# Output product of a pair of tiles with seven half-size products, and one pool of 2 KB tiles

## The chip, the cores and the metric

The kernel runs on one core of one Trainium2 chip. The metric is the time of one execution on the device in microseconds (us), measured over repeated runs. An execution taken by the hardware profiler is looked at beside it; it has a time of its own.

## What is computed

A chunked attention is followed by a gated feed-forward layer with a norm in front. All arrays are float32; the feed-forward weights arrive as raw 64-bit words and are converted on the chip.

```python
# q, k, v: 8 batches x 8 heads x 576 tokens x 64; chunks of 64 tokens
scores = scale * np.matmul(q_c, k_c.transpose(0, 1, 2, 4, 3))
attn = softmax(scores)                    # row by row
x = (attn @ v_c) laid out as 4608 tokens x 512
rms = np.sqrt(np.mean(x * x, axis=-1, keepdims=True) + 1e-06)
xn = x / rms * rms_g
g = xn @ w_gate                           # 512 -> 1536
silu = g * (1.0 / (1.0 + np.exp(-g)))
val = xn @ w_val                          # 512 -> 1536
return (silu * val @ w_out)               # 1536 -> 512
```

## The kernel before

**Precision.** A float32 operand is split into a rounded part (hi, float32r) and the rest (lo), and each product is made of three matmuls: hi x hi, hi x lo, lo x hi. A split takes a cast on ScalarE (for instance L739, `gh`) and a subtraction on VectorE (L740, `gl`).

**Tiles.** The 4608 tokens make nine tiles of 512. The first three are worked off plainly, one after the other (the loop over PLAIN). Tile 0 also converts the weights. Tile 1 also prepares seven combinations of each block of the up weights (`sides`: sums on GpSimd at L544, casts on ScalarE at L572, subtractions on VectorE at L574) and stores them in memory outside the core. In these tiles each of twelve feature blocks goes through `gated` (two up products of 12 matmuls, silu, multiplication, split at L494 and L498) and then `down` (L506). The six remaining tiles make three pairs (the loop over b at L909).

**A pair, up.** `up_pair` works off six blocks of features. For each it makes seven products (P1, P5, P6, P2, P3, P7, P4) of half-size operands that stand in for the eight of a 2 x 2 block product, at 12 matmuls each (L637), with weights from the sides and x operands `xp` of which `x_side` made the hi and lo parts (L585, L586). Behind each product, `after` combines: VectorE reads one operand from PSUM (L700, L707, L713, and others), ScalarE copies and applies silu (L679), and GpSimd adds and multiplies operands in SBUF (L701, L705, L711, L717). The result `g` of a block is 128 features x (2 x 2) x 512 tokens in SBUF.

**A pair, output.** For each of the two tiles, 12 feature blocks go through `split_g` and `down`: 12 matmuls with a piece of g stationary (128x128) and the output weights moving (512 columns). That is 24 steps, 288 matmuls and 24 splits in a pair. The four sums in PSUM of each tile are copied by `evacuate` (L730 on ScalarE, L732 on VectorE) and stored as 256 KB pieces. Splits go through two tiles of the pool `gp`; other 2 KB pieces go through a pool `tmp` of four.

**Beside it.** While a pair is worked on, the attention of the next pair's tokens runs in small steps between products: a `Steps` object calls each from a table by step number (`PAIR_STEPS`). Its stages are: loads, scores and softmax, values (L356, on PE), normalization (L370, L423, L378) and a transposition (L384). In the second half of the output the next pair's x operands are scaled (L600), subtracted from each other (`less`, L603) and split (`x_side`).

**What sets the order.** TensorE's order is written out by hand (the program order inside `manual_schedule`). The other engines' orders come from a scheduler, in which `urgent()` raises splits and combinations. Every engine works off its queue strictly in order. All transfers are issued by one queue (SP), in order. Weights come in pieces of 1 MB, asked for three ahead (AHEAD_R for the up products' `wr`, AHEAD_O for the output's `wo`); the output weights are loaded twice per pair, 12 x 1 MB.

Of the kernel before, what the change touches and what calls it, by code (L numbers as in the profile page):

```python
# [17 lines left out]
P = 128  # L18
# [45 lines left out]
def tile_chunk_attn_swiglu(  # L64
# [68 lines left out]

    def tmp_tile(name):
        return tmp.tile([P, 512], F32, tag="tmp", name=name)

# [18 lines left out]
    def conv_join(n):  # L155
        if n < len(pairs):


            low, high, w = conv[n]
            wi = w.bitcast(I32)  # L160
            nc.vector.tensor_scalar(w, w, HIGH_LEAST, HIGH_MOST, op0=ALU.max, op1=ALU.min)
            nc.vector.tensor_single_scalar(wi, wi, 3, op=ALU.logical_shift_left)
            nc.vector.scalar_tensor_tensor(
                wi, high, -(2**31), wi, op0=ALU.bitwise_and, op1=ALU.bitwise_or
            )
            nc.vector.tensor_tensor(wi, wi, low, op=ALU.add)
# [11 lines left out]
            if kind == "up":  # L178
                nc.sync.dma_start(wfd[f], w)

# [5 lines left out]

    wfd = [dram.tile([P, 2 * DM], F32, name=f"wfd{n}") for n in range(NF)]
    conv_at = [0]

# [290 lines left out]
    def gated(f, at, then):  # L480
# [35 lines left out]
    wsd = [dram.tile([P, 2, 2 * 2 * KH], F32, name=f"wsd{n}") for n in range((7 * NPR + 1) // 2)]  # L516
    wod = [dram.tile([P, 4 * DM], F32, name=f"wod{n}") for n in range(NPR)]

# [3 lines left out]
    def save_side(i, p, part):  # L522

        n = 7 * i + p
        dst = wsd[n // 2][:, n % 2].rearrange("p (a m c) -> p a m c", a=2, m=2)
        nc.sync.dma_start(dst, part.bitcast(F32))

# [3 lines left out]
    def save_plain(i):  # L531

        one, two = parts_of(2 * i), parts_of(2 * i + 1)
        save_side(i, P1, one[:, :, :, :KH])
        save_side(i, P2, one[:, :, :, KH:])
        save_side(i, P4, two[:, :, :, KH:])
        nc.sync.dma_start(wod[i], flat(out_parts[i]).bitcast(F32))

    def sides(i, st):

        at = {}

        def total(out, one, two, op):
            nc.gpsimd.tensor_tensor(out, one, two, op=op)  # L544

        def load():
            for f in range(2):
                w = st.tile([P, 2, DM], F32, tag="ab", bufs=3, name="w")
                nc.sync.dma_start(w.rearrange("p m c -> p (m c)"), wfd[2 * i + f])
                for half in range(2):  # L550
                    at[f + 1, half + 1] = w[:, :, half * KH : (half + 1) * KH]

        def sums():
            total(at[2, 2], at[2, 1], at[2, 2], ALU.add)
            total(at[2, 1], at[1, 1], at[2, 1], ALU.subtract)
            total(at[1, 1], at[2, 2], at[1, 1], ALU.subtract)
            total(at[1, 2], at[1, 2], at[1, 1], ALU.subtract)

        def split():
            save_split(i, P7, at[2, 1])  # L560
            save_split(i, P5, at[2, 2])
            save_split(i, P6, at[1, 1])
            save_split(i, P3, at[1, 2])

        return [load, sums, split]

    def save_split(i, p, w):

        n = 7 * i + p
        dst = wsd[n // 2][:, n % 2].rearrange("p (a m c) -> p a m c", a=2, m=2)  # L570
        part = tmp.tile([P, 2, KH], F32R, tag="tmp", name="side")
        nc.scalar.copy(part, w)  # L572
        nc.sync.dma_start(dst[:, 0], part.bitcast(F32))
        nc.vector.tensor_tensor(w.bitcast(F32R), w, part.bitcast(F32), op=ALU.subtract)  # L574
        nc.sync.dma_start(dst[:, 1], w)

# [13 lines left out]
    def x_sides(x1, x2, st):  # L590
# [10 lines left out]

        def less(out, one, two):
            nc.vector.tensor_tensor(out, one, two, op=sub)  # L603

# [44 lines left out]
    def up_pair(i, step, wos):  # L649
# [8 lines left out]
        for k, p in enumerate(ORD if i else FIRST):  # L658
# [4 lines left out]
            for m in range(2):  # L663
                if p == P1:
                    bank_of(m, "a", ps_h)
                elif p in (P6, P5, P4):
                    bank_of(m, {P6: "b", P5: "c", P4: "d"}[p], ps_acc)
                b = ps[m][{P1: "a", P2: "a", P6: "b", P7: "b", P5: "c", P3: "c", P4: "d"}[p]]
                product(n, m, p, b, p in (P1, P6, P5, P4), p in (P2, P7, P3, P4))
            with urgent():  # L670
# [64 lines left out]
    def split_g(src):  # L735
        gh = gp.tile([P, TT], F32R, name="gh")
        gl = gp.tile([P, TT], F32R, name="gl")
        with urgent():
            nc.scalar.copy(gh, src)  # L739
            nc.vector.tensor_tensor(gl, src, gh.bitcast(F32), op=ALU.subtract)  # L740
        return gh, gl

    def out_load(i):
        t = big([P, 2, 2, DM], F32R, "wo")
        nc.sync.dma_start(flat(t).bitcast(F32), wod[i])
        return t

    def unit_steps(u, x):
# [85 lines left out]
    for t in range(PLAIN):  # L834
        if t == 1:
# [9 lines left out]
            for i in range(NPR):  # L845
                steps = sides(i, st)
# [62 lines left out]
    for b in range(NB):  # L909
        t = PLAIN + 2 * b  # L910
        at = {}
        if b + 1 < NB:
            u = 2 * t + 4
            for n in range(4):
                for k, f in enumerate(unit_steps(u + n, (x, x2)[n // 2])):
                    at.setdefault(4 + 10 * n + PAIR_STEPS[k], []).append(f)
        step = Steps(at)
        gs = []
        wos = {}
        order = [(h, i) for h in range(2) for i in range(NPR)]  # L920
        for i in range(NPR):
            gs.append(up_pair(i, step, wos))
        loaded[0] = 0
        made = []
        if b + 1 < NB:
            made = sum(x_sides(x, x2, st), [])
        split = {}

        def split_next(n):
            if n < 2 * len(order):  # L930
                h, i = order[n // 2]
                split[n] = split_g(gs[i][:, n % 2, h])

        split_next(0)
        for n, (h, i) in enumerate(order):
            if i == 0:

                acc = [bank(ps_h if h and s < 2 else ps_acc, f"acc{s}") for s in range(NSUB)]
            for k in range(n, min(n + AHEAD_O, len(order))):
                if k not in wos:  # L940
                    wos[k] = out_load(order[k][1])
            if n == len(order) - AHEAD_R and b + 1 < NB:
                ring_load_ahead(0)
            for j in range(2):
                split_next(2 * n + j + 1)
                down(acc, 2 * i + j, *split.pop(2 * n + j), wos[n])
                step()
                if step.n > 46 and made:
                    made.pop(0)()
            if i == NPR - 1:  # L950
                for s in range(NSUB):
                    evacuate(acc, t + h, s)
        for f in made:
            f()
    ordered.__exit__(None, None, None)
# [50 lines left out]
```

## Time and profile before

| what | value |
| --- | --- |
| median of 3 runs | 935.18 us (933.87 to 935.7) |
| the profiled execution | 936.39 us |
| its span | 934.6 us |
| TensorE busy | 905.9 us, 97% of the span |
| VectorE, ScalarE, GpSimd busy | 516.2, 431.5, 172.7 us |
| granted TensorE clock | 1.000 |
| output stages of the three pairs | 62.96, 62.95 (less their first 12 matmuls) and 65.29 us |

The profiled execution lies 1.79 us above its own span, and 1.21 us above the median. In the profile an engine counts as busy while it computes. PE is TensorE's matmuls, PEld its weight loads, DVE is VectorE, ACT ScalarE, POOL GpSimd, SP the engine that issues the transfers. A row of a group reads: line, engine, operation, output<-inputs, shape, number of instructions | busy us, mean ns of one | idle us of the engine just before them and what ended it.

### The profile page before, as it was taken

The page shows a single profiled execution, that of the slowest core. Times are in us where ns is not written, and L with a number is a line of the kernel's source. Part 1 is how long each engine was busy: PE and PEld are TensorE (multiplying, and loading weights), DVE is VectorE, ACT ScalarE, POOL GpSimd, SP SyncE. Part 2 cuts the span into 40 slices and gives each one's busy share as a digit, 9 for nine tenths or more (in the row PEclk, how much of TensorE's full clock was granted, in tenths as well). Part 3 has the DMA queues.
Part 4 walks back from the last instruction along what each step waited for, and adds up shares of the span by engine and source line. Part 5 has one row for each costly group of instructions (what it writes and reads, how often), then busy time and mean ns, then how long its engine had stood idle before and what let it go on. Part 6 is the DMA issues. An engine that isn't in the chain of part 4 may idle for free.

```text
span 934.6 us, 17360 instructions
## 1 busy us (share of the span) xinstructions
PE 905.9 (97%) x6936; PEld 742.2 (79%) x6936; DVE 516.2 (55%) x889; ACT 431.5 (46%) x697; POOL 172.7 (18%) x157
## 2 busy tenths in 40 slices
PE   4599999999999999999999999999999999999998
PEld 3478788888888788888888888888888888888886
DVE  5899983554546555754664735546656332333232
ACT  4999963453446543553444425445444223222222
POOL 0100012224200000233332002322330023224100
PEclk9999999999999999999999999999999999999999
DMA  8688998868975644767789666586987585337511
GB/s 338 248 310 309 329 367 318 264 236 250 308 275 150 187 148 154 270 218 280 253 288 348 269 269 256 213 289 188 335 311 265 239 329 211 135 135 296 243 46 46
DMA packets 78737, 231.84 MB, mean 248 GB/s; under 512 B 8384, under 2 KB 40128, under 8 KB 62912
## 3 DMA queue, kind: packets, MB, share of 16 engines
q1 hardware_dynamic: 78656, 230.72, 69.0%
q8 instruction: 55, 0.90, 0.4%
q14 instruction: 26, 0.21, 0.1%
HBM read 171.97 MB, written 58.72 MB: 247 GB/s over the span
## 4 chain that ended last, share of the span: by engine, by line
PE 85%; ACT 7%; DVE 4%; DMA 2%; issue 1%; SPq 1%; POOL 0%; ACTq 0%; DVEq 0%; POOLq 0%
PE acc L506 29%; PE ps_b L637 11%; PE ps_c L637 11%; PE ps_a L637 11%; PE ps_g L471 7%; PE ps_v L471 7%; PE ps_d L637 5%; PE ps_o L356 2%; PE ps_s L239 2%; ACT w L152 1%; ACT e L275 1%; ACT raw L153 1%; ACT parts L177 1%; DVE parts L185 1%; DMA x<-kT_dram 1%
## 5 line engine op out<-in xcount | busy, mean ns | idle before, releaser
L506 PE MATMUL acc<-wo,gh 128*128 128x512 f32 x576 | 177.6, 390 | 0.0
L506 PEld LDWEIGHTS acc<-wo,gh 128*128 128x128 f32 x576 | 108.0, 188 | 22.5
L506 PE MATMUL acc<-wo,gl 128*128 128x512 f32 x288 | 112.3, 390 | 0.0
L740 DVE TENSOR_TENSOR gl<-g,gh 128x512 fp32r<-128x512 f32 x72 | 49.7, 691 | 101.2 <-ACT gh L739 99.2
L637 PE MATMUL ps_b<-xp,wr 128*128 128x512 f32 x432 | 104.7, 391 | 0.0
L637 PE MATMUL ps_c<-xp,wr 128*128 128x512 f32 x432 | 104.3, 390 | 0.0
L637 PE MATMUL ps_a<-xp,wr 128*128 128x512 f32 x432 | 103.5, 390 | 0.0
L471 PE MATMUL ps_g<-xh,parts 128*128 128x512 f32 x288 | 97.1, 396 | 1.9 <-ACT sg L489 1.4
L739 ACT CAST gh<-g 128x512 fp32r<-128x512 f32 x72 | 44.8, 623 | 116.1 <-PE acc L506 110.9
L471 PE MATMUL ps_v<-xh,parts 128*128 128x512 f32 x288 | 95.7, 392 | 0.0
L637 PEld LDWEIGHTS ps_a<-xp,wr 128*128 128x128 f32 x432 | 80.9, 188 | 16.9
L637 PEld LDWEIGHTS ps_b<-xp,wr 128*128 128x128 f32 x432 | 80.6, 188 | 17.1
L637 PEld LDWEIGHTS ps_c<-xp,wr 128*128 128x128 f32 x432 | 80.8, 188 | 16.9
L506 PE MATMUL acc<-parts,gh 128*128 128x512 f32 x288 | 90.2, 394 | 0.0
L711 POOL TENSOR_TENSOR g<-u,u 128x512 f32<-128x512 f32 x18 | 23.2, 1289 | 342.1 <-DVE u L707 244.4
L423 POOL TENSOR_TENSOR ri<-ss,mhalf 128x1 f32<-128x1 f32 x36 | 23.7, 665 | 245.1 <-DVE ss L421 244.8
L471 PEld LDWEIGHTS ps_g<-xh,parts 128*128 128x128 f32 x288 | 54.3, 189 | 14.3 <-ACT sg L489 1.8
L471 PEld LDWEIGHTS ps_v<-xh,parts 128*128 128x128 f32 x288 | 54.5, 189 | 11.3
L506 PEld LDWEIGHTS acc<-wo,gl 128*128 128x128 f32 x288 | 54.1, 188 | 11.8 <-DVE gl L740 0.5
L506 PEld LDWEIGHTS acc<-parts,gh 128*128 128x128 f32 x288 | 53.3, 188 | 11.2
L506 PE MATMUL acc<-parts,gl 128*128 128x512 f32 x144 | 56.5, 392 | 0.0
L471 PE MATMUL ps_g<-xl,parts 128*128 128x512 f32 x144 | 56.4, 391 | 0.0
(105 smaller groups left out, 1393.2 us busy)
## 6 DMA issues: line engine op xcount, KB each, us to landing
wr<-wsd SPq DMA_DIRECT2D x63, 1024.0 KB, 7.8
wo<-wod SPq DMA_DIRECT2D x36, 1024.0 KB, 8.2
raw<-w_up_dram SPq DMA_DIRECT2D x12, 1024.0 KB, 9.4
vt<-v_dram SPq DMA_DIRECT2D x18, 512.0 KB, 6.7
wsd<-parts SPq DMA_DIRECT2D x18, 512.0 KB, 6.6
out_dram<-o SPq DMA_DIRECT2D x36, 256.0 KB, 2.2
qt<-qT_dram SPq DMA_DIRECT2D x17, 512.0 KB, 5.5
kt<-kT_dram SPq DMA_DIRECT2D x17, 512.0 KB, 5.9
```

Source lines behind the costliest of these rows:

```text
L152: nc.scalar.activation(w, high.bitcast(F32), AF.Abs, scale=2.0**16)
L153: nc.scalar.mul(low, low.bitcast(U32), 2.0**-29)
L177: nc.scalar.copy(parts[:, 0].rearrange("p i c -> p (i c)"), w)
L239: nc.tensor.matmul(st["s"][j][c * CH : (c + 1) * CH, pr], st["q"][rows, pr, tok : tok + CH], st["k"][rows, pr, tok : tok + CH], start=True ...
L356: nc.tensor.matmul(st["o"][(2 * c + t) * Q : (2 * c + t + 1) * Q, h * D : (h + 1) * D], eT[c][rows, t, h], vt[rows, c, h], start=True, sto ...
L423: nc.gpsimd.tensor_tensor(ri, ss, mhalf, op=ALU.pow)
L471: nc.tensor.matmul(ps, a[f][:, cols], b[dt], start=(dt == 0 and i == 0), stop=(dt == NDT - 1 and i == 2),)
L506: nc.tensor.matmul(acc[s], a[:, cols], b, start=(f == 0 and i == 0), stop=(f == NF - 1 and i == 2),)
L637: nc.tensor.matmul(ps, w[:, a, m, cols], xp[:, b, kt], start=start and kt == 0 and i == 0, stop=stop and kt == 1 and i == 2, skip_group_ch ...
L711: nc.gpsimd.tensor_tensor(g[:, 0, 1], kp["u2"], kept[0]["u2"], op=mult)
L739: nc.scalar.copy(gh, src)
L740: nc.vector.tensor_tensor(gl, src, gh.bitcast(F32), op=ALU.subtract)
```

## The change

**Output of a pair.** `down_pair` takes the place of `down` for the pairs. It makes the output product with seven half-size products too: 7 products x 6 blocks are 42 steps (n = 6p + i for product p and block i), each with two halves m and 3 matmuls, 252 matmuls in a pair. The output weights are now stationary (128x128, features of the output on partitions) and the split g moves (512 tokens). `down_after` combines the products: copies on ScalarE, four kinds of sums on VectorE from PSUM, one on GpSimd. The output is stored transposed in 8 pieces of 256 KB, and the host turns it back.

**Operands.** Each step splits one operand (cast L779, subtraction L780), two steps ahead (AHEAD_G). Behind the splits of P1, P5, P6 and P2, GpSimd writes the next operand over g in place (L809): 24 subtractions of 128x512 per pair.

**Pool.** One pool `tmp` of eight 2 KB tiles serves sg, gh, gl, o, side and the second half's u2 and p5, where there were two pools of (2 x 2) and 4.

**Output weights.** Tile 0 also stores the converted output weights (`wfo`), tile 2 makes their sides (`out_sides`: 4 sums of 128x256 on GpSimd, 4 casts, 4 subtractions and 8 stores for each of 6 blocks), and a pair loads them as 11 pieces of up to 1 MB.

**Beside it.** The units' steps come two steps earlier (2 + 10n for 4 + 10n), the x operands' at steps 44, 46, ..., and two of their subtractions of 128x1024 go from VectorE to GpSimd.

```diff
-    gp = ctx.enter_context(tc.tile_pool(name="gp", bufs=2))
-    tmp = ctx.enter_context(tc.tile_pool(name="tmp", bufs=4))
+    tmp = ctx.enter_context(tc.tile_pool(name="tmp", bufs=8))
...
     def split_g(src):
-        gh = gp.tile([P, TT], F32R, name="gh")
-        gl = gp.tile([P, TT], F32R, name="gl")
+        gh = tmp_tile("gh", F32R)
+        gl = tmp_tile("gl", F32R)
...
+    def down_pair(b, gs, wos, step):
...
+        sums = {P1: ((0, 0), (0, 1)), P5: ((0, 0), (1, 1)), P6: ((0, 1), (1, 1)), P2: ((1, 0), (0, 0))}
+        homes = {P1: (0, 0), P5: (0, 0), P6: (0, 0), P2: (1, 0), P3: (1, 1), P7: (0, 1), P4: (1, 0)}
...
+        def split_next(n):
+            if n >= 7 * NPR:
+                return
+            p, i = divmod(n, NPR)
+            g = gs[i]
+            split[n] = split_g(g[:, homes[p][0], homes[p][1]])
+            if p in sums:
+                (j, h), (j1, h1) = sums[p]
+                nc.gpsimd.tensor_tensor(g[:, j, h], g[:, j1, h1], g[:, j, h], op=ALU.subtract)
...
+        for n in range(AHEAD_G):
+            split_next(n)
+        for n in range(7 * NPR):
+            p, i = divmod(n, NPR)
+            for k in range(n // 4, min(n // 4 + AHEAD_O, NOS)):
+                if k not in wos:
+                    wos[k] = out_load(k)
...
+            for m in range(2):
...
+                for k, (a, c) in enumerate(((0, 0), (0, 1), (1, 0))):
+                    nc.tensor.matmul(
+                        ps[m][INTO[p]],
+                        w[:, a, m * P : (m + 1) * P],
+                        parts[c],
...
+            split_next(n + AHEAD_G)
+            if i == NPR - 1:
+                with urgent():
+                    for m in range(2):
+                        down_after(p, m, ps[m], kept[m], store)
+            step()
...
+            lambda: less(b12, b22, b12, nc.gpsimd),
             lambda: x_side(P6, t1),
+            lambda: less(b21, t1, b21, nc.gpsimd),
             lambda: x_side(P3, b22),
-            lambda: less(b12, b22, b12),
             lambda: x_side(P7, b12),
-            lambda: less(b21, t1, b21),
             lambda: x_side(P4, b21),
...
+            for i in range(NPR):
+                for k, f in zip((4, 6, 7), out_sides(i)):
+                    at.setdefault(3 * i + k, []).append(f)
```

**GpSimd's queue, end of the first pair's up products and start of its output.** The names are g (a block's result, six of them), u2, p5 and p1 (partial sums of the last block), ri (the norm of a unit). Before:

```order
L711 TENSOR_TENSOR g_5092<-u2_5150,u2_5148 128x512
L701 TENSOR_TENSOR p5_5130<-p1_5107,p5_5130 128x512
L701 TENSOR_TENSOR p5_5132<-p1_5109,p5_5132 128x512
L705 TENSOR_TENSOR g_5092<-p5_5132,p5_5130 128x512
L717 TENSOR_TENSOR g_5092<-p1_5109,p1_5107 128x512
L423 TENSOR_TENSOR ri_5349<-ss_5346,mhalf_99 128x1
L423 TENSOR_TENSOR ri_5356<-ss_5353,mhalf_99 128x1
L711 TENSOR_TENSOR g_5815<-u2_5891,u2_5889 128x512
```

After (L751, L741, L745, L757 and L427 are L711, L701, L705, L717 and L423 of before):

```order
L809 TENSOR_TENSOR g_4085<-g_4085 128x512 x2
L809 TENSOR_TENSOR g_4283<-g_4283 128x512
L809 TENSOR_TENSOR g_4557<-g_4557 128x512
L809 TENSOR_TENSOR g_4283<-g_4283 128x512
L809 TENSOR_TENSOR g_4557<-g_4557 128x512
L751 TENSOR_TENSOR g_5277<-u2_5352,u2_5350 128x512
L741 TENSOR_TENSOR p5_5332<-p1_5292,p5_5332 128x512
L741 TENSOR_TENSOR p5_5334<-p1_5294,p5_5334 128x512
L745 TENSOR_TENSOR g_5277<-p5_5334,p5_5332 128x512
L809 TENSOR_TENSOR g_4802<-g_4802 128x512 x2
L427 TENSOR_TENSOR ri_5484<-ss_5481,mhalf_96 128x1
L427 TENSOR_TENSOR ri_5491<-ss_5488,mhalf_96 128x1
```

The first six of the new sums stand ahead of the last block's sums and multiplications, and the others follow one upon the other, where before the queue went on to the next pair.

**VectorE's queue in the middle of the first pair's output.** xp is an x operand, x2 and t1 are what it is made of. Before:

```order
L740 TENSOR_TENSOR gl_5497<-g_4819,gh_5496 128x512
L600 TENSOR_SCALAR x2_2642<-x2_2642,g_col_98 128x8x64 x3
L740 TENSOR_TENSOR gl_5515<-g_5092,gh_5514 128x512
L603 TENSOR_TENSOR t1_5251<-x2_2642,x_127 128x1024
L600 TENSOR_SCALAR x2_2642<-x2_2642,g_col_98 128x8x64
L603 TENSOR_TENSOR x2_2642<-x2_2642 128x8x128
L586 TENSOR_TENSOR xp_5549<-t1_5251,xp_5549 128x1024
L740 TENSOR_TENSOR gl_5534<-g_5092,gh_5533 128x512
```

After (L780, L641, L644 and L627 are L740, L600, L603 and L586 of before):

```order
L641 TENSOR_SCALAR x2_2668<-x2_2668,g_col_95 128x8x64 x2
L780 TENSOR_TENSOR gl_5739<-g_5277,gh_5738 128x512
L644 TENSOR_TENSOR t1_5514<-x2_2668,x_124 128x1024
L780 TENSOR_TENSOR gl_5752<-g_4085,gh_5751 128x512
L641 TENSOR_SCALAR x2_2668<-x2_2668,g_col_95 128x8x64 x2
L627 TENSOR_TENSOR xp_5756<-t1_5514,xp_5756 128x1024
L780 TENSOR_TENSOR gl_5766<-g_4283,gh_5765 128x512
L855 TENSOR_TENSOR u2_5770<-ps_b_5694,p1_5609 128x512
L855 TENSOR_TENSOR u2_5772<-ps_b_5698,p1_5611 128x512
L780 TENSOR_TENSOR gl_5781<-g_4557,gh_5780 128x512
```

The subtraction `x2<-x2` has left VectorE's queue, and reads of PSUM (L855) have come between the splits.

More of the change, by code (lines that the diff above doesn't have):

```diff
@@ L187, in tile_chunk_attn_swiglu @@
     wfd = [dram.tile([P, 2 * DM], F32, name=f"wfd{n}") for n in range(NF)]
+    wfo = [dram.tile([P, 2 * DM], F32, name=f"wfo{n}") for n in range(NPR)]
     conv_at = [0]
@@ L516, in tile_chunk_attn_swiglu @@
     wsd = [dram.tile([P, 2, 2 * 2 * KH], F32, name=f"wsd{n}") for n in range((7 * NPR + 1) // 2)]
-    wod = [dram.tile([P, 4 * DM], F32, name=f"wod{n}") for n in range(NPR)]
+    NOS = (7 * NPR + 3) // 4
+    wod = [dram.tile([P, 4, 2 * KH], F32, name=f"wod{n}") for n in range(NOS)]
     def flat(t):
@@ L536, in save_plain, with out_side, sides @@
         save_side(i, P4, two[:, :, :, KH:])
-        nc.sync.dma_start(wod[i], flat(out_parts[i]).bitcast(F32))
-    def sides(i, st):
+        for p, j, half in (P1, 0, 0), (P2, 1, 0), (P4, 1, 1):
+            part = out_parts[i][:, :, j, half * KH : (half + 1) * KH]
+            nc.sync.dma_start(out_side(i, p), part.bitcast(F32))
+    def out_side(i, p):
+        n = NPR * p + i
+        return wod[n // 4][:, n % 4].rearrange("p (a c) -> p a c", a=2)
+    def sides(i, load, place, blocks_of):
@@ L541, in sides, with begin, sums, split @@
         at = {}
         def total(out, one, two, op):
-            nc.gpsimd.tensor_tensor(out, one, two, op=op)
+            nc.gpsimd.tensor_tensor(at[out], at[one], at[two], op=op)
+        def begin():
+            at.update(blocks_of(load()))
+        def sums():
+            total((2, 2), (2, 1), (2, 2), ALU.add)
+            total((2, 1), (1, 1), (2, 1), ALU.subtract)
+            total((1, 1), (2, 2), (1, 1), ALU.subtract)
+            total((1, 2), (1, 2), (1, 1), ALU.subtract)
+        def split():
+            for p, k in (P7, (2, 1)), (P5, (2, 2)), (P6, (1, 1)), (P3, (1, 2)):
+                w, dst = at[k], place(i, p)
+                n = 1
+                for d in w.shape[1:]:
+                    n *= d
+                part = tmp_tile("side", F32R)[:, :n]
+                if len(w.shape) == 3:
+                    part = part.rearrange("p (m c) -> p m c", m=2)
+                nc.scalar.copy(part, w)
+                nc.sync.dma_start(dst[:, 0], part.bitcast(F32))
+                nc.vector.tensor_tensor(w.bitcast(F32R), w, part.bitcast(F32), op=ALU.subtract)
+                nc.sync.dma_start(dst[:, 1], w)
@@ L546, in load, with up_sides @@
+        return [begin, sums, split]
+    def up_sides(i, st):
         def load():
-            for f in range(2):
-                w = st.tile([P, 2, DM], F32, tag="ab", bufs=3, name="w")
+            ws = [st.tile([P, 2, DM], F32, tag="ab", bufs=3, name="w") for _ in range(2)]
+            for f, w in enumerate(ws):
                 nc.sync.dma_start(w.rearrange("p m c -> p (m c)"), wfd[2 * i + f])
-                for half in range(2):
-                    at[f + 1, half + 1] = w[:, :, half * KH : (half + 1) * KH]
@@ L553, in sums @@
[L553 to L575, printed above, removed]
+            return ws
@@ new lines, in blocks_of, with out_sides, load @@
+        def blocks_of(ws):
+            return {
+                (f + 1, half + 1): w[:, :, half * KH : (half + 1) * KH]
+                for f, w in enumerate(ws)
+                for half in range(2)
+            }
+        return sides(i, load, side, blocks_of)
+    def out_sides(i):
+        def load():
+            w = big([P, 2, DM], F32, "w")
+            nc.sync.dma_start(w.rearrange("p j c -> p (j c)"), wfo[i])
+            return w
+        def blocks_of(w):
+            return {
+                (half + 1, j + 1): w[:, j, half * KH : (half + 1) * KH]
+                for j in range(2)
+                for half in range(2)
+            }
+        return sides(i, load, out_side, blocks_of)
@@ L600, in scale, with less @@
                 nc.vector.tensor_scalar(x[:, :, dt], x[:, :, dt], col, None, op0=ALU.mult)
-        def less(out, one, two):
-            nc.vector.tensor_tensor(out, one, two, op=sub)
+        def less(out, one, two, engine=nc.vector):
+            engine.tensor_tensor(out, one, two, op=sub)
         return [
@@ L735, in split_g @@
     def split_g(src):
[L736 to L737 removed]
+        gh = tmp_tile("gh", F32R)
+        gl = tmp_tile("gl", F32R)
         with urgent():
@@ L845, in tile_chunk_attn_swiglu @@
             for i in range(NPR):
-                steps = sides(i, st)
+                steps = up_sides(i, st)
                 made[max(2 * i - 1, 0)].append(steps[0])
@@ L915, in tile_chunk_attn_swiglu @@
                 for k, f in enumerate(unit_steps(u + n, (x, x2)[n // 2])):
-                    at.setdefault(4 + 10 * n + PAIR_STEPS[k], []).append(f)
+                    at.setdefault(max(2 + 10 * n + PAIR_STEPS[k], 0), []).append(f)
         step = Steps(at)
-        gs = []
         wos = {}
-        order = [(h, i) for h in range(2) for i in range(NPR)]
-        for i in range(NPR):
-            gs.append(up_pair(i, step, wos))
+        gs = [up_pair(i, step, wos) for i in range(NPR)]
         loaded[0] = 0
-        made = []
         if b + 1 < NB:
[L926 to L954, printed above, removed]
+            for n, f in enumerate(sum(x_sides(x, x2, st), [])):
+                at.setdefault(44 + 2 * n + 2 * (n > 3), []).append(f)
+        down_pair(b, gs, wos, step)
     ordered.__exit__(None, None, None)
@@ L1003 @@
     rows = res.results[0]["out_dram"]
+    pairs = rows[PLAIN * TT :].reshape(NB, DM, 2 * TT).transpose(0, 2, 1).reshape(-1, DM)
+    rows = np.concatenate([rows[: PLAIN * TT], pairs])
     turned = rows[2 * TT :].reshape(-1, 4, 2, Q, DM).transpose(0, 2, 1, 3, 4).reshape(-1, DM)
```

71 lines of the change are left out of this document (59 added, 12 removed).

## The prediction

> **What bounds the kernel now.** I read the page first, then the table of stretches, then the chain of waits, and last the groups and single lines of the operations that the change adds.
>
> ```profile
> span 934.6 us, 17360 instructions
> PE 905.9 (97%) x6936; PEld 742.2 (79%) x6936; DVE 516.2 (55%) x889; ACT 431.5 (46%) x697; POOL 172.7 (18%) x157
> ```
>
> TensorE (PE) is busy for 97% of the span; no other engine passes 55%. The next table has four stretches: the third plain tile, then the output products of the three pairs (start:end, length, then busy time and count of each engine).
>
> ```profile
> core 0: us, PE busy (x) PEld busy (x) DVE busy (x) ACT busy (x) POOL busy (x), PEclk, DMA share, GB/s
> 272.00:368.00 96.00, 94.72 (x1074) 77.32 (x1074) 49.38 (x101) 45.41 (x66) 4.33 (x8) 1.00 0.53 157
> 496.50:560.00 63.50, 63.50 (x294) 52.32 (x280) 33.94 (x45) 24.28 (x38) 1.10 (x2) 1.00 0.75 290
> 688.00:751.20 63.20, 63.20 (x301) 52.09 (x286) 33.89 (x45) 23.92 (x37) 1.10 (x2) 1.00 0.66 252
> 865.40:930.90 65.50, 65.31 (x289) 53.76 (x287) 18.59 (x27) 15.67 (x27) 2.08 (x2) 1.00 0.25 101
> ```
>
> In the three output stages PE never pauses and the granted clock is 1.00: there the number of matmuls is the time. Two more things matter later. VectorE (DVE) is half busy in them, and GpSimd (POOL) does almost nothing: 1.10, 1.10 and 2.08 us.
>
> The chain in order of time (start, length, what) gives the price of a matmul.
>
> ```profile
> 368.01 5.44 PE ps_a L637 x24
> ...
> 496.64 62.96 PE acc L506 x276
> ...
> 688.24 62.95 PE acc L506 x276
> ...
> 865.43 65.29 PE acc L506 x288
> ```
>
> 65.29 us for 288 matmuls are 0.2267 us each, the same as 5.44 / 24 in the up products. A step of the new output stage (2 m x 3 matmuls) will be 6 x 0.2267 = 1.36 us, and one up product (12) 2.72 us.
>
> **Part 1: fewer matmuls.** Seven half-size products need 7 x 6 x 2 x 3 = 252 matmuls for a pair instead of 288. The shape stays: 128x128 stationary, 512 columns moving. Each pair saves 36 x 0.2267 = 8.2 us, three pairs 24.5 us, all of it on the path that sets the end. An output stage without a wait would take 252 x 0.2267 = 57.1 us.
>
> **Part 2: splits and sums.** PE now needs a new pair gh, gl every 1.36 us, where it needed one every 2.72 us (12 matmuls). There are 42 splits in a pair, not 24, and behind 24 of them GpSimd writes a sum over its operand.
>
> ```profile
> L740 DVE TENSOR_TENSOR gl<-g,gh 128x512 fp32r<-128x512 f32 x72 | 49.7, 691 | 101.2 <-ACT gh L739 99.2 <-PE acc L506 2.0
> L739 ACT CAST gh<-g 128x512 fp32r<-128x512 f32 x72 | 44.8, 623 | 116.1 <-PE acc L506 110.9 <-DVE g L694 3.1 <-POOL g L717 2.2
> L701 POOL TENSOR_TENSOR p<-p,p 128x512 f32<-128x512 f32 x36 | 46.6, 1293 | 24.8 <-DVE p L700 15.4 <-DMA wr<-wsd 8.4
> ```
>
> By these rows each engine alone keeps up: ScalarE needs 0.62 us a step, VectorE 0.69, GpSimd 1.29, all under 1.36. What decides is whether VectorE and GpSimd can work at the same time. The output stages of before cannot tell, since GpSimd rests there. The stretch in which the plain tiles prepare weight sums can: GpSimd adds (L544) there while VectorE subtracts (L498, L574). The next rows have min/median/max in ns.
>
> ```profile
> L498 DVE TENSOR_TENSOR gl<-sg,gh x36: 676/691/1221, 49.4 to 364.1; 128x512 fp32r<-128x512 f32 x36
> L574 DVE TENSOR_TENSOR w<-w,side x24: 649/684/1777, 161.9 to 254.0; 128x512 fp32r<-128x512 f32 x24
> L544 POOL TENSOR_TENSOR w<-w x24: 1276/1291/1694, 142.1 to 246.7; 128x512 f32<-128x512 f32 x24
> L713 DVE TENSOR_TENSOR p<-p,ps_d x36: 686/687/689, 387.1 to 865.5; 128x512 f32<-128x512 f32 x36
> L701 POOL TENSOR_TENSOR p<-p,p x36: 1280/1294/1299, 385.1 to 863.5; 128x512 f32<-128x512 f32 x36
> ```
>
> VectorE's subtractions with both operands in SBUF stretch from 0.69 to 1.22 and 1.78 us there, GpSimd's sums from 1.29 to 1.69. L713, which reads one operand from PSUM, never moves (686 to 689) although GpSimd's L701 works at the same times. Here is one such meeting.
>
> ```profile
> 244.26 1.20 DVE L498 TENSOR_TENSOR gl<-sg,gh 128x512 fp32r<-128x512 f32 x1 [0.69 <-ACT gh L494]
> 244.99 2.98 POOL L544 TENSOR_TENSOR w<-w 128x512 f32<-128x512 f32 x2
> ```
>
> The subtraction should have ended at 244.95 and ended at 245.46; two sums took 2.98 us instead of 2 x 1.291 = 2.58, so VectorE held GpSimd up for 0.40. The two take turns: of a split's 0.69 us, 0.40 shut GpSimd out, and while GpSimd adds, the split stands still. A step with a split and a sum then needs 1.29 + 0.40 = 1.69 us of their common access, against 1.36 us on PE. (The Trainium skill, page "SBUF — State Buffer", section "SBUF: two separate sides", says that VectorE with two SBUF inputs and GpSimd share one pair of ports, an exclusive lock for the whole instruction. The stretched rows agree that they exclude each other; the 0.40 does not agree with the whole instruction, by which a turn would be 1.98 us.)
>
> How far that reaches: at most four splits are in flight, since gh and gl take two of eight tiles, so PE's lead is three steps, 4.1 us. The sums of P5 come behind all others that matter, and step 12 + i needs the sum of P5 on block i. I count from the first split (after P6 of the last up block, four products ahead of the output) to the 26th, where GpSimd has done all. PE covers 4 x 2.72 us of up products, less 1.31 for the first cast and subtraction, and 25 x 1.36 = 34.0 of output steps. In pairs 1 and 2 a unit's values lie there too:
>
> ```profile
> 495.16 1.48 PE L356 MATMUL ps_o<-vt,eT 64*32 64x64 f32 x128
> ```
>
> Cover: 10.9 - 1.3 + 1.5 + 34.0 = 45.1 us there, 43.6 in pair 3. In the same time GpSimd has 24 sums and five operations of the last up block, 29 x 1.29 = 37.4. Pairs 1 and 2 also make the next pair's x operands then:
>
> ```profile
> L586 DVE TENSOR_TENSOR xp<-x,xp 128x1024 fp32r<-128x1024 f32 x15 | 18.1, 1213 | 1.9 <-ACT xp L585 1.7
> L603 DVE TENSOR_TENSOR x<-x 128x1024 f32<-128x1024 f32 x3 | 3.7, 1226 | 0.1
> L600 DVE TENSOR_SCALAR x<-x,g_col x24: 432/479/889, 325.1 to 712.5; 128x512 f32<-128x512 f32 x24
> ```
>
> Two subtractions of 1024 columns move to GpSimd; at twice 1.29 each (an estimate) they are 5.2 us. VectorE keeps 26 splits, 26 x 0.40 = 10.4; eight operations of 1024 columns at 1.22 less the 0.29 that a split did not hold (0.69 - 0.40), 8 x 0.93 = 7.4; four scalings at 0.48 - 0.29, 0.8. Sum: 37.4 + 5.2 + 10.4 + 7.4 + 0.8 = 61.2, against 45.1: 16.1 us lost in each of pairs 1 and 2, if the turns follow without a gap. For gaps:
>
> ```profile
> L423 POOL TENSOR_TENSOR ri<-ss,mhalf x36: 547/550/1950, 18.1 to 690.6; 128x1 f32<-128x1 f32 x36
> L378 ACT ACTIVATE xu<-xu,ri 128x512 f32<-128x512 f32 x28 | 19.2, 719 | 8.6 <-POOL ri L423 8.5
> L384 DVE STREAM_TRANSPOSE xu<-xu 128x1024 f32<-128x1024 f32 x14 | 17.4, 1245 | 18.1 <-ACT xu L378 18.1
> ```
>
> ri, scaling and transposition of the last unit stand between the sums, 0.55 + 0.72 + 1.25 = 2.5 us, and four reads of PSUM on VectorE, 4 x 0.69 = 2.8, let GpSimd run but no split: up to 5.3 more, 21.4. I take 20, near the upper end, because the queues are in order and the turns will not pack tightly. Pair 3 has no unit and no x work: 37.4 + 10.4 = 47.8 against 43.6 is 4.2, with the PSUM reads up to 7.0; I take 6. Total 2 x 20 + 6 = 46; ends 2 x 16.1 + 4.2 = 36.4 and 2 x 21.4 + 7.0 = 49.8. A gain is no end here: no removed work of VectorE or GpSimd lies in that stretch.
>
> **Part 3: what costs little.** The third plain tile now makes the sides of the output weights: 24 sums of 256 columns, 24 casts, 24 subtractions, six loads, 48 stores of 128 KB. PE idles there for 1.3 us in all (96.00 - 94.72), some of it here:
>
> ```profile
> PE ps_o L356 <- DMA eT<-away_e: 1.3, 2, 1.1
> wo<-wod SPq DMA_DIRECT2D x36, 1024.0 KB, 8.2
> ```
>
> VectorE's 49.38 and ScalarE's 45.41 us of 96 have room for it, and turns of 24 half-length sums (0.65 each, an estimate from 1.29) with gated splits stay inside a block's 5.44 us. With sg, side, gh and gl in one pool, a split can now also wait for a side's store. I take +1 for all this, between 0 and the 8 of the rival below. The units come two steps earlier, with the same matmuls on PE: nothing. Output weights come as 1 MB for each 5.44 us of PE's time (four steps), as before (24 matmuls); at 8.2 us to land and three ahead they hide. 42 casts of 0.62 are 26 us of ScalarE in 57. The last pair ends as now with a copy and a store of 256 KB: nothing.
>
> **Sum.** The profiled execution took 936.39 us (span 934.6 and 1.79 around it), 1.21 above the median of the runs. 936.39 - 24.5 + 46 + 1 = 958.9; less 1.21, **957.7 us**. With the ends 36.4 and 49.8, and 0 to 4 for the third tile, 947 to 964.5.
>
> **Rivals.**
> *A, faster.* The sums slip into the time in which VectorE does not read two operands from SBUF, and the lead of three steps takes up the rest. For it: over a whole output stage common access in pair 3 is 37.4 + 42 x 0.40 = 54.2 us against 10.9 + 57.1, so it fits if spread evenly. Against it: VectorE's and GpSimd's queues both hold ready work at the front, and turns serve them alike. Losses of 1 to 8 us in all give 935.2 - 24.5 + 1 + (1 to 8) = 912.7 to 919.7. The point from which it decides: a loss under 8.2 us per pair. Chance 0.17.
> *B, slower in the third plain tile.* All transfers go through one queue, in order. The 48 new stores stand ahead of eT in it, as the 1.1 us wait for eT shows in small; 2 us for each of four units are 8 more than 957.7: 965.7. PE would idle for about 9 us in that tile. Chance 0.05.
> *C, each shuts the other out for its full length.* A turn is 1.29 + 0.69 = 1.98. Pairs 1 and 2: 42.6 + 26 x 0.69 + 8 x 1.22 + 4 x 0.48 = 72.2 less 45.1, 27; pair 3: 37.4 + 17.9 - 43.6 = 11.7. Total 66 instead of 46: 977. The 0.40 speaks against. (That is what the rule of the page "SBUF — State Buffer" in the Trainium skill, same section, would make of this kernel.) Chance 0.05.
> *D, no change:* losses happen to equal 24.5. Chance 0.03.
>
> **How the numbers follow.** The forecast has 0.70. Slower by over 0.2% (1.9 us, about what a measurement of this kernel can tell from no change): 0.70 + 0.05 + 0.05 = 0.80; within: 0.03; faster: 0.17. The forecast's own range is 947 to 964.5. The range to hold 8 in 10 adds B, C and D, and leaves out A: 934 to 977.
>
> **What would show it.** In the profile after, the output stages of pairs 1 and 2 should last about 57 + 20 = 77 us, pair 3's 63, with PE waiting for gl; gl should average over 1.0 us while sums run, and the sums 1.6 to 1.7 instead of 1.29. In the last third of each stage, behind the sums, splits should be back at 0.69 and PE without waits. The forecast is wrong if sums and splits overlap at 1.29 and 0.69, if PE's waits end on a cast or a transfer, or if the loss per pair stays under 8.2 us.

## The result, and the profile after

| | time (us) | against the kernel before |
| --- | --- | --- |
| forecast | 957.7 (934 to 977) | slower, chance 0.80 |
| measured, median of 4 runs | 975.06 (971.41 to 976.92) | 1.0424, 95% interval 1.0389 to 1.0459 |
| the kernel before beside it | 935.12 (933.87 to 935.7) | |

The change is slower by 4%. The time lies inside the stated range, but above the forecast's own 947 to 964.5. Here are the page's first lines of the profile after.

```profile
span 975.1 us, 17703 instructions
PE 909.4 (93%) x6828; PEld 725.5 (74%) x6828; DVE 630.4 (65%) x973; ACT 484.1 (50%) x789; POOL 335.2 (34%) x265
```

PE has the 108 matmuls less (6828 for 6936), but now it is idle or slowed for 7% of the span. The table of stretches shows where: the second and third plain tile, then up products and output of pair 1, the output of pair 2, and the output of pair 3.

```profile
core 0: us, PE busy (x) PEld busy (x) DVE busy (x) ACT busy (x) POOL busy (x), PEclk, DMA share, GB/s
165.80:273.20 107.40, 105.51 (x824) 85.74 (x817) 58.81 (x107) 52.39 (x82) 29.25 (x24) 1.00 0.84 267
273.20:383.00 109.80, 103.60 (x1090) 83.87 (x1090) 59.72 (x128) 55.33 (x93) 22.86 (x32) 0.95 0.75 230
383.00:510.60 127.60, 126.66 (x1274) 103.28 (x1273) 84.10 (x149) 65.42 (x97) 51.39 (x42) 1.00 0.80 284
510.60:589.40 78.80, 64.82 (x254) 47.63 (x253) 66.67 (x66) 36.26 (x59) 45.06 (x27) 0.96 0.55 197
...
715.50:794.40 78.90, 66.25 (x254) 48.53 (x253) 66.68 (x66) 36.31 (x59) 45.41 (x28) 0.94 0.49 181
...
908.70:971.40 62.70, 61.44 (x253) 45.85 (x251) 50.37 (x48) 28.06 (x47) 38.67 (x25) 1.00 0.21 86
```

From the first matmul to the end of the last, the three output stages took 78.9, 79.1 and 62.8 us; I had forecast 77, 77 and 63. Before, the same stages took 67.3 and 67.3 (the last unit's values among them) and 65.4. That makes 20.9 us more. The other 19.7 of the 40.6 us between the two spans lie elsewhere: first tile +1.4, second +3.4 (104.0 before), third +10.3 (99.5 before), up products of pairs 1 and 2 +3.1 and +1.6. In the last two, 1.5 us each is the unit's values, which the steps moved there out of the output.

The groups of the splits and sums, after (xcount | busy, mean ns):

```profile
L780 DVE TENSOR_TENSOR gl<-g,gh 128x512 fp32r<-128x512 f32 x126 | 143.6, 1176 | 28.1 <-POOL g L745 14.5 <-ACT gh L779 12.5
L809 POOL TENSOR_TENSOR g<-g 128x512 f32<-128x512 f32 x72 | 117.4, 1653 | 46.3 <-DVE gl L780 45.3
L779 ACT CAST gh<-g 128x512 fp32r<-128x512 f32 x126 | 76.3, 621 | 83.3 <-PE ps_c L831 16.8 <-POOL g L751 16.7 <-DVE gl L780 15.5
```

A split takes 1176 ns for 691, a sum 1653 for 1293, so they do hold each other up. But the right-hand side holds something that the prediction had not named: splits and casts also stood idle until GpSimd's last-block operations (L745, L751) were done. PE's waits in the output of pair 1 (total us, times, longest us):

```profile
PE ps_a L831 <- DVE gl L780: 8.2, 7, 2.2
PE ps_a L831 <- ACT gh L779: 2.9, 1, 2.9
PE ps_c L831 <- DVE gl L780: 2.7, 2, 2.2
```

Most of them end on gl, as forecast, but one long wait ends on a cast (gh), and so does one of 3.2 us in pair 2; the prediction had named that as a sign against it. Experiment 6 shows where it comes from.

### The profile page after: what moved, and what is told of

Its sections match the earlier page's. It is cut to its first block, busy times and chain, and to the rows that moved or that the text cites. A ratio compares the mean times of both kernels' runs of the same rounds, so it can differ in the third digit from the quotient of the medians.

```text
span 975.1 us, 17703 instructions
## 1 busy us (share of the span) xinstructions
PE 909.4 (93%) x6828; PEld 725.5 (74%) x6828; DVE 630.4 (65%) x973; ACT 484.1 (50%) x789; POOL 335.2 (34%) x265
## 4 chain that ended last, share of the span: by engine, by line
PE 61%; DVE 11%; POOL 8%; DMA 7%; ACT 7%; issue 4%; SPq 1%; DVEq 0%; ACTq 0%; POOLq 0%
PE ps_b L678 10%; PE ps_a L678 9%; PE ps_c L678 9%; PE ps_g L475 5%; PE ps_v L475 5%; PE acc L510 4%; PE ps_d L678 4%; PE ps_b L831 4%; POOL g L809 4%; DVE gl L780 3%; PE ps_c L831 3%; PE ps_d L831 2%; DMA x<-away_x 2%; DVE xp L627 2%; POOL w L559 2%
## 5 line engine op out<-in xcount | busy, mean ns | idle before, releaser
L780 DVE TENSOR_TENSOR gl<-g,gh 128x512 fp32r<-128x512 f32 x126 | 143.6, 1176 | 28.1 <-POOL g L745 14.5
L809 POOL TENSOR_TENSOR g<-g 128x512 f32<-128x512 f32 x72 | 117.4, 1653 | 46.3 <-DVE gl L780 45.3
L779 ACT CAST gh<-g 128x512 fp32r<-128x512 f32 x126 | 76.3, 621 | 83.3 <-PE ps_c L831 16.8
L427 POOL TENSOR_TENSOR ri<-ss,mhalf 128x1 f32<-128x1 f32 x36 | 23.9, 680 | 235.5 <-DVE ss L425 233.6
L559 POOL TENSOR_TENSOR w<-w 128x512 f32<-128x512 f32 (+1 forms) x48 | 50.8, 1061 | 117.8 <-DMA w<-wfo 31.5
L751 POOL TENSOR_TENSOR g<-u,u 128x512 f32<-128x512 f32 x18 | 23.2, 1292 | 147.3 <-ACT u L719 109.6
L497 DVE TENSOR_TENSOR sg<-ps_v,sg 128x512 f32<-128x512 f32 x36 | 24.7, 686 | 68.8 <-PE ps_v L475 47.0
L728 DVE TENSOR_TENSOR u<-ps_b,p 128x512 f32<-128x512 f32 x36 | 24.9, 691 | 66.0 <-PE ps_b L678 65.9
L475 PE MATMUL ps_g<-xl,parts 128*128 128x512 f32 x144 | 57.3, 398 | 1.2 <-DVE xl L450 1.2
```

Source lines behind the costliest of these rows:

```text
L427: nc.gpsimd.tensor_tensor(ri, ss, mhalf, op=ALU.pow)
L475: nc.tensor.matmul(ps, a[f][:, cols], b[dt], start=(dt == 0 and i == 0), stop=(dt == NDT - 1 and i == 2),)
L497: nc.vector.tensor_tensor(sg, pv, sg, op=ALU.mult)
L559: nc.gpsimd.tensor_tensor(at[out], at[one], at[two], op=op)
L728: nc.vector.tensor_tensor(kp["u2"], b["b"], kp["p1"], op=add)
L751: nc.gpsimd.tensor_tensor(g[:, 0, 1], kp["u2"], kept[0]["u2"], op=mult)
```

## The experiments

Each kernel ran beside the kernel before on one chip. Stage lengths are from the first to the last matmul of a stage in the trace.

**1. No sums.**

```diff
-                nc.gpsimd.tensor_tensor(g[:, j, h], g[:, j1, h1], g[:, j, h], op=ALU.subtract)
```

> The changed kernel without GpSimd's 24 sums per pair (the operands of four of the seven products are then not formed; everything else stays, splits and matmuls too). Theory of turns: with the sums gone GpSimd seldom holds VectorE up; the splits fall back from a mean of 1.18 us to about 0.72, and the output stages from 78.9, 79.1 and 62.8 us to about 62, 62 and 58 (57.1 without any wait; the two 1024-column subtractions and the five operations of the last block still take turns in pairs 1 and 2). Time about 975 - 17 - 17 - 5 = 936. Rival, lead: only four splits in flight are too few for one split per 1.36 us; then the stages stay above 70 us and PE still waits for gl or gh. Rival, ScalarE: casts come late; then PE's waits end on gh.

One run: 936.85 us. Output stages 60.9, 61.5, 57.3 us:

```profile
511.70:572.50 60.80, 59.30 (x254) 46.71 (x253) 47.49 (x60) 33.62 (x53) 11.16 (x6) 1.00 0.70 248
698.60:760.00 61.40, 59.83 (x254) 46.59 (x253) 48.95 (x65) 35.53 (x58) 11.97 (x7) 1.00 0.65 236
874.10:931.30 57.20, 57.20 (x253) 47.09 (x251) 33.57 (x47) 26.88 (x45) 5.50 (x4) 1.00 0.24 95
```

In the third row PE is busy without a pause. The lead of four splits and ScalarE's casts are therefore enough, and both rivals fall. The sums are to blame for 18.0 + 17.6 + 5.5 = 41 of the 49.5 us that the three stages lay above 57.1. This run does not tell why: taking turns, or merely standing in GpSimd's queue.

**2. The sums on VectorE.**

```diff
-                nc.gpsimd.tensor_tensor(g[:, j, h], ...
+                nc.vector.tensor_tensor(g[:, j, h], ...
```

> The changed kernel with the 24 sums of each pair on VectorE in place of GpSimd (the two 1024-column subtractions stay on GpSimd). Theory of turns: a sum takes 0.69 us instead of 1.65, nothing shuts the splits out, so a step with split and sum costs VectorE 2 x 0.69 = 1.38 us, just above PE's 1.36. Pair 3 has nothing else to do: about 59 us. Pairs 1 and 2 add about 13 us of x operands and norms to VectorE's 66 x 0.69 = 45.5: about 64 us. Time about 975 - 15 - 15 - 4 = 941. Rival, GpSimd was not the cause and VectorE's own load is: then 24 more subtractions on VectorE make the stages longer than 79 and 63 us, and the time is over 975.

Measured 947.86 us, ratio 1.0131 (1.0116 to 1.0146); output stages 66.6, 68.3 and 59.0 us, against 64, 64 and 59. The expectation was 941; the granted clock was 0.97 and 0.92 in the first two stages, which had not been counted. More work on the fuller engine made the kernel 27 us faster, so VectorE's load was not what the stages waited for.

**3. The kernel before with the sides and the pool.** The diff is the change without `down_pair`: `wfo` stores, `out_sides`, the pool of eight.

> The kernel before with the rest of the change alone: the converted output weights stored in the first tile, their sides made in the third, and the one pool of 2 KB tiles; the pairs' output products stay as they were and do not use the new sides. My prediction's sum has 1 us for this: 936. The profile of the changed kernel shows its up products of the first pair 15 us later than before, 10 of it in the third tile: if that comes from the sides, this kernel takes about 950, and PE waits there for eT about 4 us in all and then runs at half clock for some 3.4 us at a time. If instead the plain tiles suffered from something in the pairs' part (order, slots of the weights), it stays at 936.

Measured 951.08 us, ratio 1.0160 (1.0141 to 1.0179), 15.2 us slower than the kernel before beside it. The third tile:

```profile
273.60:381.20 107.60, 101.21 (x1090) 82.37 (x1090) 58.47 (x125) 55.42 (x93) 22.70 (x32) 0.98 0.73 231
```

The pairs' new output has no part in this: making the sides and sharing the tiles cost 15 us by themselves, where I had put 1.

**4. Fills instead of sums.**

```diff
-                nc.gpsimd.tensor_tensor(g[:, j, h], g[:, j1, h1], g[:, j, h], op=ALU.subtract)
+                for _ in range(2):
+                    nc.gpsimd.memset(g[:, j, h], 0.5)
```

> The changed kernel with each of GpSimd's 24 sums per pair replaced by two fills of the same 128x512 piece with a constant (the operands' values are lost; order and waits stay). GpSimd then is busy and writes SBUF, but reads nothing there. If VectorE is shut out only by GpSimd's reading, the splits stay near 0.69 to 0.75 us and the output stages near 62, 62, 58 us as without sums. If any use of SBUF by GpSimd shuts VectorE out, the splits stretch by the length of a fill, and the stages lie between those and 79, 79, 63 us, in the measure of the fills' length.

One run: 938.91 us; stages 63.9, 63.9 and 57.3. The group of the fills (its min/median/max), pair 3's stretch, and two rows of it in time:

```profile
L810 POOL MEMSET g<- x144: 523/527/806, 401.4 to 905.3; 128x512 f32 x144
```

```profile
876.20:933.30 57.10, 57.10 (x253) 47.03 (x251) 33.54 (x47) 27.21 (x45) 21.81 (x35) 1.00 0.24 95
```

```profile
519.42 1.29 DVE L780 TENSOR_TENSOR gl<-g,gh 128x512 fp32r<-128x512 f32 x2
519.55 4.28 POOL L810 MEMSET g<- 128x512 f32 x8
```

GpSimd is busy for 21.81 us in pair 3, yet PE does not pause. Eight fills run on end in 4.28 us (8 x 0.53), and two splits beneath them take 1.29, no longer than alone. Over all 126 splits the mean is 805 ns here and 787 without sums (experiment 1), against 1176 with them:

```profile
L780 DVE TENSOR_TENSOR gl<-g,gh 128x512 fp32r<-128x512 f32 x126 | 98.9, 805 | 43.4 <-ACT gh L779 33.7 <-POOL g L745 9.4
L780 DVE TENSOR_TENSOR gl<-g,gh 128x512 fp32r<-128x512 f32 x126 | 97.0, 787 | 43.2 <-ACT gh L779 36.1 <-POOL g L745 6.8
```

So VectorE is not shut out by GpSimd being busy or writing, but by its reading of operands. (So says the Trainium skill, page "SBUF — State Buffer", section "SBUF: two separate sides": two SBUF inputs on VectorE exclude only a GpSimd operation that reads SBUF. This run agrees.) The fills are shorter than the sums, 1.07 to 1.29 us, and the order did not stay quite the same: in pair 1 the fills of three sums, not six sums, stand ahead of L751. So a part of the difference between 78.9 and 63.9 may be queue and not turns.

**5. The sides made in the first pair's up products.** `out_sides` goes into the steps of pair 1, one block each five products, stores two steps behind.

> The changed kernel with the sides of the output weights made during the first pair's up products instead of the third tile (one block each five products, its eight stores asked for two steps behind its subtractions, so that the transfer queue never waits for them). Theory that the queue is what the third tile loses by: PE's waits for eT there go back from 4.1 to about 1.3 us, the three half-clock periods of 3.41 us go with them, and the tile takes about 99.5 us instead of 109.8; the up products have spare time on every engine and stay near 126 us. Time about 975 - 10 = 965, output stages still 79, 79, 63. Rival: the loss is due to the load itself (transfers, casts, subtractions) and only moves: the first pair's up products get about 10 us longer and the time stays at 975.

Measured 980.45 us, ratio 1.0474 (1.0442 to 1.0505). The third tile and the up products of pair 1:

```profile
272.50:371.70 99.20, 98.17 (x1090) 80.18 (x1089) 52.19 (x107) 48.59 (x70) 5.02 (x9) 1.00 0.54 168
371.70:516.80 145.10, 133.74 (x1274) 106.66 (x1273) 94.21 (x169) 72.69 (x120) 74.61 (x67) 0.96 0.86 298
```

The third tile is cured, 99.2 us as forecast, so the sides made there are its loss. But the up products are 17 us longer: the waits there now end on weights (`wr`), and the mean DMA share is 0.86. The rival, that the load only moves, was nearer to the time (975, against 965 by the theory), but it had the up products 10 us longer, not 17.

**6. Own tiles.** Two tiles for gh, two for gl and four for the rest in place of eight in common; splits use the two kinds by turns.

```diff
-        gh = tmp_tile("gh", F32R)
-        gl = tmp_tile("gl", F32R)
+        gh = tmp_tile("gh", F32R, "gh" if n % 2 else "tmp")
+        gl = tmp_tile("gl", F32R, "gl" if n % 2 else "tmp")
```

> The changed kernel with the eight 2 KB tiles parted again: two for gh, two for gl, four for the rest; in the pairs splits use the two kinds by turns, so that four are in flight as before. If gated splits of the plain tiles wait for tiles that sides hold until they are stored, the first two tiles lose the 5 us that they lost against the kernel before (the third tile then starts at about 268 instead of 273 us) and the third some of its 10; time about 968. If the pool has no part in it, everything stays: 975, third tile from 273.

One run: 959.38 us, 16 us better than the changed kernel's median, for parting the same eight tiles:

```profile
268.30:374.80 106.50, 101.11 (x1090) 81.92 (x1089) 59.13 (x127) 52.74 (x91) 20.64 (x30) 0.98 0.73 232
507.40:579.80 72.40, 63.58 (x254) 48.41 (x253) 64.36 (x60) 33.46 (x53) 38.35 (x21) 0.95 0.56 201
705.90:780.20 74.30, 63.81 (x254) 48.47 (x253) 65.76 (x65) 35.75 (x58) 41.72 (x25) 0.95 0.54 196
894.40:953.80 59.40, 59.17 (x253) 46.42 (x251) 49.66 (x47) 26.79 (x45) 35.47 (x22) 1.00 0.23 91
```

The second tile is back at its old length (the third starts at 268.3), as expected. What I had not expected are the output stages: 72.5, 74.4 and 59.5, that is 6.4, 4.7 and 3.3 less. The changed kernel's rows at the start of the first output (which begins at 510.55) show what the splits waited for:

```profile
499.67 8.34 POOL L809 TENSOR_TENSOR g<-g 128x512 f32<-128x512 f32 x6 [7.14 <-DVE gl L780]
507.97 1.30 POOL L751 TENSOR_TENSOR g<-u,u 128x512 f32<-128x512 f32 x1
509.21 2.55 POOL L741 TENSOR_TENSOR p<-p,p 128x512 f32<-128x512 f32 x2
511.84 1.29 POOL L745 TENSOR_TENSOR g<-p,p 128x512 f32<-128x512 f32 x1
```

```profile
509.30 0.62 ACT L779 CAST gh<-g 128x512 fp32r<-128x512 f32 x1 [5.55 <-POOL g L751]
```

```profile
498.91 2.98 DVE L780 TENSOR_TENSOR gl<-g,gh 128x512 fp32r<-128x512 f32 x3
513.16 0.69 DVE L780 TENSOR_TENSOR gl<-g,gh 128x512 fp32r<-128x512 f32 x1 [6.08 <-POOL g L745]
521.38 5.16 DVE L780 TENSOR_TENSOR gl<-g,gh 128x512 fp32r<-128x512 f32 x3
```

Three splits are done by 501.9. The fourth needs the common tiles that the last block's u2 and p5 hold. GpSimd gives them free only behind six of the new sums that stand ahead in its queue (order fence in the change): the cast waits until L751 ends, the subtraction until L745 ends at 513.1. PE does not need it before 514.6, so this split itself comes in time. But VectorE's queue has stood still for 6.08 us ahead of it, and behind it come the last unit's steps: L374 on VectorE at 513.77, the norm (L427) on GpSimd behind two more sums, the scaling (L382) on ScalarE at 517.14. The fifth cast stands behind L382 in ScalarE's queue and starts at 518.38; for it PE waits 2.89 us, until 519.04. From 521 on, the turns rule: three splits in 5.16 us are 1.72 each, against 1.36 on PE.

Two things blur this run. With the tiles parted, the scheduler put two of the new sums, not six, ahead of the last block's multiplication, so tiles and order are not told apart; VectorE's idle time until L745 (here L746) fell from 14.5 to 6.8 us over the three outputs. And in the up products of pair 1 PE stood still once for 2.55 us with no wait that the profile shows and then ran at half clock for 3.41 us (experiment 1 has the same stop); the up products took 132.8 us, 5.1 more than in the changed kernel, which gave the first splits more time ahead of the output. So the 6.4 us of pair 1 may not all be the tiles'. The up products of pairs 2 and 3 kept their lengths, and there 4.7 and 3.3 us went.

**7. Sums on VectorE and sides in the up products.** Both edits, and the two 1024-column subtractions back on VectorE.

> Both cures together: the sums of each pair and the two 1024-column subtractions on VectorE, and the output weights' sides made during the first pair's up products. GpSimd then only meets VectorE in the last block's five operations. From the 947.9 of sums on VectorE alone: about 10 less in the third tile, and the x operands' subtractions at 1.22 on VectorE in place of 2.6 to 3.9 on GpSimd with VectorE shut out, about 2 less in each of pairs 1 and 2: 934, level with the kernel before. If VectorE's own load is what sets 66 and 68 us, the output stages stay there and the time is 938.

Measured 945.98 us, ratio 1.0115 (1.0074 to 1.0157), where I expected 934: the up products of pair 1 took 150.8 us, as in the fifth run for want of weights. Output stages 58.0, 63.1 and 59.0.

**8. Sums on VectorE and own tiles** (with the sides in the third tile again).

> The sums and the two 1024-column subtractions on VectorE, and the eight 2 KB tiles parted (two gh, two gl, four for the rest); the sides of the output weights stay in the third tile. If the tiles held by the last block's partial sums and by unstored sides cost some 16 us beside the turns, as the run with parted tiles alone showed (959 instead of 975), and turns the rest, the output stages come to about 60, 61 and 58 us and the third tile starts at 268: about 935 - 24.5 + 3 x 3 + 8 (third tile) + 3 = 930. If parting the tiles only helps where GpSimd is slow, the stages stay at 63 to 66 and the time at 940.

Measured 931.0 us, ratio 0.9951 (0.9935 to 0.9967): faster than the kernel before.

```profile
269.70:380.60 110.90, 102.96 (x1090) 83.07 (x1089) 60.16 (x130) 52.96 (x91) 20.52 (x30) 0.97 0.73 224
506.70:568.40 61.70, 59.06 (x254) 47.00 (x253) 57.90 (x85) 36.05 (x58) 5.85 (x5) 1.00 0.70 252
694.40:756.00 61.60, 59.25 (x254) 46.88 (x253) 57.83 (x85) 35.82 (x58) 5.31 (x5) 1.00 0.66 237
870.20:927.60 57.40, 57.40 (x253) 46.97 (x251) 43.99 (x65) 27.13 (x45) 5.45 (x4) 1.00 0.23 94
```

VectorE works 57.9 us in 61.7, and PE pauses for 2.6. With turns and shared tiles gone the 24.5 us of saved matmuls show, less the third tile's 11 and the 9.6 us by which the three stages still lie above 57.1 each. Against experiment 7, the outputs of pairs 2 and 3 are 1.4 and 1.5 us shorter: that much the parted tiles are worth there when the sums are on VectorE.

**9. Late stores.** As 8, each block's eight stores of sides one step later.

> As the kernel with own tiles and all sums on VectorE, and in the third tile each block's eight stores of output sides are asked for one step behind their subtractions. If the transfer queue waits for the casts and subtractions behind which it stores, and eT comes late by that, the third tile loses 5 us less (102 instead of about 107) and the time falls by about 5. If the loss there comes from the transfers themselves or from the engines' work, nothing changes.

Measured 932.02 us, ratio 0.9969 (0.9955 to 0.9983): nothing gained; the third tile took 109.8, at a mean granted clock of 0.95. PE's waits in this kernel and, in the tenth (below), ScalarE's row ahead of its one long wait:

```profile
PE ps_g L477 <- ACT sg L495: 10.3, 2, 8.8
PE ps_o L362 <- DMA eT<-away_e: 0.3, 1, 0.3
```

```profile
307.00 1.28 ACT L495 ACT_TABLE_LOAD   x1 [2.55 <-DMA wod<-side]
```

The waits for eT fell from 4.6 us to 0.3, as the theory of the queue has it, but PE now waits up to 8.8 us for silu's result. By the second row ScalarE stands idle for 2.55 us ahead of that silu until a store of a side lets go of one of the four tiles; why the wait is longer than this, the row does not show. One wait took the other's place.

**10. Scaling on ScalarE.** As 9, the x operands' scaling by `nc.scalar.mul`.

> As the one with late stores, and the scaling of the x operands by the norm's weights on ScalarE instead of VectorE. It takes eight operations of about 0.5 to 0.7 us off VectorE per pair. If VectorE's load still sets the output stages of pairs 1 and 2, each gets 2 to 3 us shorter and the time falls by 5; if PE's own 57.1 us are nearly reached, less than 2.

Measured 930.41 us, ratio 0.9951 (0.9936 to 0.9966). The output stages fell by 0.9 and 0.6 us to 61.1 and 61.1, and the time by 1.6, as in the second case; but its reason does not hold, since 61.1 is still 4 us above PE's own 57.1.

**11. Packed sides.** As 10, two sides of 1 KB in one 2 KB tile.

> As the one with scaling on ScalarE, and two output sides of 1 KB each share one of the four 2 KB tiles, so that a block's four sides hold two tiles instead of all four until they are stored. If silu's tile is what the one long wait in the third tile (7.9 us for sg) is for, that wait goes and the third tile falls from 109.5 to about 102 us, the time from 930.4 to about 923. If the casts and subtractions themselves keep ScalarE from the silu, the wait stays and so does the time.

Measured 929.1 us, ratio 0.9942 (0.9930 to 0.9954), the fastest here. The long wait for sg is gone (1.0 us), but the third tile took 106.8, not 102, since waits for eT came back. Its mean clock was 0.98, where it was 0.95 in the tenth run (109.5 us); that alone is about 3 us (an estimate), as much as the tile gained:

```profile
PE ps_o L362 <- DMA eT<-away_e: 6.5, 3, 4.4
```

## Why the prediction was right and where it failed

The direction and the main cost were right. That 975.06 lies in the stated range is owed to the room left for rivals B and C.

**Part 1** held: in pair 3 without sums the stage takes 57.3 us, 57.1 forecast.

**Part 2** held in size. Loss forecast 20 + 20 + 6 = 46, measured 21.8 + 22.0 + 5.7 = 49.5. Its mechanism held in part. Turns are shown: sums with a median of 1.73 us (1.69 forecast), splits of 1.72 us under sums, hardly any stretch under fills (experiment 4).

```profile
L809 POOL TENSOR_TENSOR g<-g x72: 1277/1728/2244, 499.7 to 945.9; 128x512 f32<-128x512 f32 x72
```

(The rule of the whole instruction, on the page "SBUF — State Buffer" of the Trainium skill, section "SBUF: two separate sides", would have given 1.98 a turn; the median does not reach it, and rival C's 27 and 11.7 us did not come.) The meeting from which I took the 0.40 was shown too short: the two sums of its row begin at 244.99, when the subtraction should have been over, and what held it was the sum ahead of them, which began at 243.62. The 0.40 came out all the same (1.73 - 1.29 = 0.44). Behind the sums the splits are back at 0.69 in pair 1 from 568 us on, and PE does not wait any more, as forecast.

Three things are in the loss that the prediction did not have. The first is the wait for tiles: 14.4 of the 49.5 us went when the tiles were parted (with the reservations of experiment 6), and the prediction had them all as turns. I had counted four splits in flight, and that GpSimd has the last block's five operations to do. But u2 and p5 hold two tiles of the same pool, so it was three, and the fourth waits for operations that stand behind six sums. The second is that this wait seems dear only together with the sums on GpSimd: with fills, on the same shared tiles, the stages lay 3.0, 2.4 and 0 us above those without sums, and with the sums on VectorE the parted tiles gained 1.4 and 1.5 us. The third is the clock: its means of 0.96 and 0.94 in the outputs of pairs 1 and 2 are about 3 and 5 us (an estimate from the table of stretches). That my allowance for gaps, 46 - 36.4 = 9.6 us, stood in for all this was luck.

**Part 3** failed: "I take +1 for all this, between 0 and the 8 of the rival below". It measured 15.2 us alone (experiment 3), beyond the 8 too. I compared busy times with the tile's length, which says nothing of queues in order. The mechanism was rival B's, as a part: in the third tile PE waits for eT as B has it, though for 4.1 us where B had about 9, and for silu besides.

```profile
PE ps_o L360 <- DMA eT<-away_e: 4.1, 4, 1.5
PE ps_g L475 <- ACT sg L493: 2.1, 1, 2.1
```

These are 4.9 us more than the 1.3 of before. The rest of the tile's 10.3 us is the clock, which no step had: a mean of 0.95 over 109.8 us is about 5 us (an estimate).

```profile
311.86 0.27 PE L360 MATMUL ps_o<-vt,eT 64*32 64x64 f32 x2 [1.53 <-DMA eT<-away_e]
313.03 2.41 PE L360 MATMUL ps_o<-vt,eT 64*32 64x64 f32 x126 [0.90 <-DMA eT<-away_e]
```

126 small matmuls take 2.41 us behind two waits, where 122 took 1.43 before. This part varies from run to run: the same tile took 106.5 us at 0.98 in experiment 6 and 106.25 us at 1.00 in experiment 2 (from 270.80 on).

The second tile's 3.4 us go with the common pool (experiment 6: it is back at its old length with own tiles). Forecast 957.7 and measured 975.06 differ by 17.4: 14.2 of it is part 3 (15.2 by experiment 3, for 1) and 3.5 part 2.

**Open.** The third tile's 7 to 11 us, of which the clock took up to 5, went away only when the sides left it, and came back in the up products. Whether the number of transfers or their place in the one queue sets the price there was not parted: late stores and packed sides each ended one wait and woke another. In experiment 6, tiles and order were not parted either.

## What to carry to other kernels

Where VectorE subtracts two operands from SBUF, a GpSimd sum of operands in SBUF beside it is no free work: here 24 sums a pair on GpSimd cost 41 us in the three outputs, and with them on the fuller VectorE the kernel was 27 us faster. Pools merged into one can hand each user the waits of the others, so ask for each tile who frees it, and what stands ahead of that on its engine. Price added side work in a stage with small waits by the queues that it joins, not by busy shares.

## What the runs showed of the hardware that was not expected

- Waits of 1.53 and 0.90 us with two small matmuls between them came just before a lower clock: 0.50 from 312.7 us on, for 3.41 us (the small matmuls took 2.41 us where 1.43 is usual). In the outputs of pairs 1 and 2, where no wait of PE is over 3.2 us, the mean clock was 0.96 and 0.94, and single matmuls took up to 797 ns for 389:

```profile
L831 PE MATMUL ps_a<-gl,wo x72: 389/389/797, 510.8 to 946.2; 128*128 128x512 f32 x72
```

- A fill on GpSimd (0.53 us for 128x512) hardly holds VectorE up: the splits averaged 805 ns with fills beside them, 787 with neither fills nor sums and 1176 with sums.
